# One eviction for two half banks, and a longer stretch for the preparation of later batches, in a fused attention and feed-forward kernel

## Chip, cores, metric

The kernel runs on one core of a Trainium2 chip. The metric is the device time of one execution in microseconds (us), as the median of several runs. A profile page comes from one of them.

## The reference, cut

```python
B, N, C = 4, 6080, 256              # attention over channels, four batches
qn = q / (norm(q, axis=1) + 1e-6);  kn = k / (norm(k, axis=1) + 1e-6)
s  = kn.transpose(0, 2, 1) @ qn / tau            # "gram" product, 256 x 256 per batch
a  = softmax(s, axis=-1)
x  = v @ a                                       # 24320 x 256
h  = x @ w_in                                    # 256 -> 2048
g  = s_ * relu(h)**2 + b_
out = g @ w_out                                  # 2048 -> 256
```

## The kernel before

The kernel folds `a @ w_in` into one matrix `wa` per batch, so that a group of 512 rows needs `v @ wa`, relu, square and the product with `w_out`. There are 48 groups, and each takes 16 passes of the main loop, which this text calls **half-slots**. A half-slot issues two matmuls of 512 columns for group g and seven of 128 columns for group g - 1.

The product with `w_out` is done with seven quarter products in place of eight (a scheme like Strassen's). Four of them (1, 3, 5, 7) accumulate in one half of a PSUM bank called X, and the bank YZ holds Y in one half and Z in the other. VectorE evicts a partial sum (reads it out of PSUM) after each product. The code is cut, and the comments are added:

```python
        def p1():                                   # after product 1 (bank X)
            st["u1"] = U()
            evacuate(st["u1"], st["X"], rowconst[:, lo], 1)
        def p5():                                   # after product 2 (half Z)
            st["u5"] = U()
            evacuate(st["u5"], st["Z"], rowconst[:, hi], 1)
        def p6():                                   # after product 3 (bank X, accumulated)
            st["u2"] = U()
            evacuate(st["u2"], st["X"], rowconst[:, hi], 1)
        def p2():                                   # after product 4 (half Y)
            evacuate(out_sb(0, lo), st["Y"], st["u1"], 2)
        def p7():                                   # after product 5 (bank X)
            evacuate(out_sb(1, hi), st["X"], st["u5"], 2)
        def p3():                                   # after product 6 (half Z, accumulated)
            evacuate(out_sb(0, hi), st["Z"], st["u2"], 2)
            ...
        def p4():                                   # after product 7 (bank X)
            evacuate(out_sb(1, lo), st["X"], rowconst[:, lo], 1)
            ...
        products = [
            ("X", G(0, 0), W[:, 0, :, lo], p1),
            ("Z", lambda: S[1], T1, p5),
            ("X", lambda: S[2], T2, p6),            # may start only when p1 has read X
            ("Y", G(1, 0), W[:, 1, :, lo], p2),
            ("X", lambda: S[3], T3, p7),
            ("Z", lambda: S[4], W[:, 1, :, hi], p3),
            ("X", G(1, 1), N4, p4),
        ]
```

VectorE also makes the operand sums S1 to S4, and three quarters of the squares (`g<-r`); each of these instructions takes 1.2 us. The places within a group of 16 half-slots are fixed. Counted in half-slots from the start of group g, for the products of group g - 1: S1 at 2, S2 at 3, p1 at 5, S3 at 6, p5 at 7, p6 at 9, S4 at 10, p2 at 12, p7 at 14, p3 at 16, p4 at 18. The squares of VectorE stand at 8, 12 and 16, those of ScalarE at 3 and 5. A place 16 is place 0 of the next group.

Between these, batches 1 to 3 are prepared while the batch before is computed. The gram product of a batch takes 12 chunks of 4 pairs of matmuls. Each chunk brings one ScalarE square and, on VectorE, a square (`sq<-qk`) and two folds (`f<-sq`, `f<-f`). Then 18 finishing steps make `wa` (code cut, comments added):

```python
    FIN = (0, 3, 5, 7, 9, 11, 13, 17, 19, 22)   # copy, norms, 4 x inverse, scale, exp, exp, sums
    for b in range(1, B):
        gr = grams[b]
        w0 = first_group[b - 1] * FT + (26 if b == 1 else 6)
        w1 = first_group[b] * FT - 3
        fin_len = 54
        span = (w1 - fin_len) - w0 - 12
        n = NCH * JC
        for c in range(NCH):
            sc = w0 + span * c * JC / n
            ...
            for j in range(JC):
                at_step(w0 + span * (c * JC + j) / n, lambda gr=gr, c=c, j=j: gr.mm(c, j))
            def norm_step(gr=gr, c=c, sc=sc):
                ops = gr.norm_ops(c)             # ScalarE square, VectorE square, two folds, add
                for i, f in enumerate(ops):
                    at_step(int(sc) + 2 + 1 + i * 3, f)
            at_step(sc + 1, norm_step)
        ...                                      # the finishing steps start at w1 - fin_len + 1
```

## Time and profile before

| | before |
|---|---|
| time, median of 6 runs | 718.98 us |
| span of the profiled run | 717.3 us |
| TensorE busy | 695.1 us (97%) |
| VectorE busy | 623.7 us (87%), 877 instructions |
| ScalarE busy | 545.1 us (76%) |
| stops of TensorE in the main loop | 2.67 us (VectorE 1.08, ScalarE 1.59) |

A **stop**, here and below, is the time by which two successive matmul starts lie further apart than is usual for the shape of the first (0.056, 0.109 and 0.216 us for 128, 256 and 512 columns); all such excesses above 0.015 us are added up from the first matmul of the main loop on. A stop is put down to the engine whose instruction released the second matmul.

### The profile page before, as it was taken

What the parts mean: (1) busy time and instruction counts of PE and PEld (TensorE: products, weight loads), DVE (VectorE), ACT (ScalarE), POOL (GpSimd) and SP (SyncE); (2) the same over time, 40 slices, a digit from 0 to 9 for tenths busy, and PEclk for the clock granted to TensorE, in tenths of its full rate; (3) what the DMA queues carried; (4) which work ended last, traced back from release to release, by engine and by line L of the source; (5) the groups of instructions that cost most, each with busy time, mean ns of one, the idle gap of its engine ahead of it and who ended that gap; (6) DMA issues with size and microseconds to landing.
All of it is one profiled execution on the core that took longest, in us unless ns stands there. A gap on an engine that the chain in (4) does not pass through costs nothing.

```text
span 717.3 us, 17484 instructions
## 1 busy us (share of the span) xinstructions
PE 695.1 (97%) x7417; PEld 502.9 (70%) x7417; DVE 623.7 (87%) x877; ACT 545.1 (76%) x593; POOL 110.7 (15%) x189
## 2 busy tenths in 40 slices
PE   4599999999999999999999999999999999999998
PEld 2456777776677777777677777777668777777777
DVE  4879999988789999998889899998887888888886
ACT  5779877787777777778777778777877777777875
POOL 4532323102101222111010222110000000000000
PEclk9999999999999999999999999999999999999999
DMA  9999999636555988444763887953323333321201
GB/s 235 208 258 173 151 154 160 112 100 123 116 109 118 135 137 144 110 91 90 132 149 59 139 141 122 152 94 75 100 63 75 93 71 75 96 60 45 83 31 74
DMA packets 87198, 83.47 MB, mean 116 GB/s; under 512 B 56304, under 2 KB 62000, under 8 KB 87120
## 3 DMA queue, kind: packets, MB, share of 16 engines
q0 software_dynamic: 26352, 43.40, 38.5%
q1 hardware_dynamic: 60192, 37.64, 21.9%
q8 instruction: 58, 0.95, 0.6%
q10 hardware_dynamic: 576, 1.31, 0.5%
q14 instruction: 20, 0.16, 0.1%
HBM read 78.91 MB, written 24.90 MB: 145 GB/s over the span
## 4 chain that ended last, share of the span: by engine, by line
PE 92%; DMA 4%; DVE 2%; ACT 2%; issue 0%; DVEq 0%; ACTq 0%
PE h_ps L661 45%; PE o_ps L829 40%; PE s_ps L148 4%; PE wa_ps L329 2%; DMA qk<-in_k_dram 1%; DMA raw<-in_q_dram 1%; DMA w_in<-in_moe_w_in_dram 1%; PE o_ps L733 1%; ACT sq L177 1%; ACT r L671 1%; DVE f L191 1%; PE o_ps L707 0%; DVE sq L174 0%; DVE o_sb L689 0%; DVE S L758 0%
## 5 line engine op out<-in xcount | busy, mean ns | idle before, releaser
L671 ACT ACTIVATE r<-h_ps 128x1024 f16<-128x1024 f32 (+1 forms) x384 | 388.3, 1014 | 151.2 <-PE h_ps L661 147.5
L661 PE MATMUL h_ps<-vT,wa 128*128 128x512 f16 (+7 forms) x1632 | 452.0, 364 | 0.5 <-ACT r L671 0.4
L829 PEld LDWEIGHTS <-S 128*128 128x128 f16 x2944 | 198.0, 98 | 84.7 <-issue 0.2
L829 PEld LDWEIGHTS <-g 128*128 128x128 f16 x2208 | 155.1, 98 | 74.1
L684 DVE TENSOR_TENSOR g<-r 128x2048 f16<-128x2048 f16 (+2 forms) x150 | 174.6, 1164 | 14.5 <-ACT r L671 13.9
L829 PE MATMUL o_ps<-T,S 128*128 128x128 f16 x2208 | 183.3, 219 | 0.1
L661 PEld LDWEIGHTS <-wa 128*128 128x128 f16 x1632 | 136.0, 98 | 20.3 <-DVE wa L324 0.7
L829 PE MATMUL o_ps<-w_out,g 128*128 128x128 f16 x1472 | 134.2, 219 | 0.2 <-DVE u L689 0.2
L689 DVE SCALAR_TENSOR_TENSOR o_sb<-o_ps,s_out,u 128x256 f32<-128x256 f32 x138 | 66.3, 481 | 50.9 <-PE o_ps L829 48.7
L682 ACT ACTIVATE g<-r 128x1024 f16<-128x1024 f16 (+1 forms) x97 | 100.4, 1035 | 0.2
L148 PE MATMUL s_ps<-qk 128*128 128x256 f16 (+1 forms) x384 | 70.2, 283 | 16.0 <-ACT qk L139 9.5
L388 POOL DMA_DIRECT2D v<-in_v_dram x48 | 30.9, 648 | 264.9 <-DMA vT<-v 197.7
L689 DVE SCALAR_TENSOR_TENSOR u<-o_ps,s_out,rowconst 128x256 f32<-128x256 f32 x138 | 65.7, 476 | 0.0
L829 PE MATMUL o_ps<-w_out,S 128*128 128x128 f16 x736 | 63.5, 219 | 0.0
L829 PE MATMUL o_ps<-N,g 128*128 128x128 f16 x736 | 63.4, 219 | 0.0
L207 POOL DMA_DIRECT2D f<-f x30 | 26.3, 876 | 224.4 <-DVE f L191 182.5
L758 DVE TENSOR_TENSOR S<-S,g 128x2048 f16<-128x2048 f16 (+1 forms) x47 | 56.4, 1200 | 1.3
L177 ACT ACTIVATE sq<-qk 128x1024 f16<-128x1024 f16 (+2 forms) x53 | 54.5, 1041 | 3.9 <-DMA qk<-in_k_dram 2.3
L756 DVE TENSOR_TENSOR S<-g 128x2048 f16<-128x2048 f16 (+1 forms) x47 | 56.0, 1192 | 0.0
L762 DVE TENSOR_TENSOR S<-g,S 128x2048 f16<-128x2048 f16 x46 | 55.9, 1214 | 0.0
L760 DVE TENSOR_TENSOR S<-g 128x2048 f16<-128x2048 f16 x46 | 55.8, 1214 | 0.0
L148 PEld LDWEIGHTS <-qk 128*128 128x128 f16 (+1 forms) x384 | 32.2, 101 | 22.0 <-ACT qk L139 10.0
(85 smaller groups left out, 313.8 us busy)
## 6 DMA issues: line engine op xcount, KB each, us to landing
out_dram<-o_sb SPq DMA_DIRECT2D x42, 512.0 KB, 3.0
v<-in_v_dram POOLq DMA_DIRECT2D x47, 256.0 KB, 4.6
qk<-in_k_dram POOLq DMA_DIRECT2D x42, 256.0 KB, 6.2
qk<-in_q_dram POOLq DMA_DIRECT2D x42, 256.0 KB, 7.1
f<-f POOLq DMA_DIRECT2D x30, 128.0 KB, 3.2
vT<-v SPq DMA_TRANSPOSE x182, 3.1
out_dram<-o_sb SPq DMA_DIRECT2D x10, 256.0 KB, 4.5
w<-in_moe_w_out_dram POOLq DMA_DIRECT2D x4, 512.0 KB, 9.6
```

The lines of the kernel that those rows point to most:

```text
L148: po(nc.tensor.matmul(self.s_ps[:, ch, :], qc[:np_, j, ts(ch, P)], kc[:np_, j, :], start=(c == 0 and j == 0 and ch == 0), stop=(c == len(s ...
L177: po(nc.scalar.activation(out=st["sq"][:np_, a, js, :], in_=(qc, kc)[a][:np_, js, :], func=AF.Square))
L661: po(nc.tensor.matmul(dst, wa[:, ci, ts(m, P)], src, start=(ci == 0), stop=(ci == CH - 1), skip_group_check=True))
L671: po(nc.scalar.activation(out=r16[:, :, i % 2, :n], in_=h_tiles.pop((g, i))[:, :, :n], func=AF.Relu))
L682: po(nc.scalar.activation(out=dst, in_=src, func=AF.Square))
L684: po(nc.vector.tensor_mul(dst, src, src))
L689: po(nc.vector.scalar_tensor_tensor(out=dst, in0=src, scalar=s_out, op0=ALU.mult, in1=add, op1=ALU.add))
L756: po(nc.vector.tensor_add(T[1], A21, A22))
L758: po(nc.vector.tensor_sub(T[2], T[1], A11))
L760: po(nc.vector.tensor_sub(T[3], A11, A21))
L762: po(nc.vector.tensor_sub(T[4], A12, T[2]))
L829: po(nc.tensor.matmul(st[name][:, j, :], a()[:, i, ts(j, P)], w[:, i, :], start=first, stop=last, skip_group_check=True))
```

## The change

Two things are meant to relieve VectorE, which is 87% busy. First, Y and Z are evicted together, as one bank of 512 elements after product 6, which saves one instruction per group; the u buffers are widened for that, and a fold of batch 0 takes its buffer from another pool. Second, the finishing steps of batches 1 to 3 start ten half-slots later (54 becomes 44), batch 1 starts four later (26 becomes 30), and the gram products and their squares and folds are spread over the longer stretch.

```diff
--- before.py
+++ after.py
@@ -75,7 +75,7 @@
     rpool = pool("rpool", 2)
     gpool = pool("gpool", 2)
     spool = pool("spool", 1)
-    upool = pool("upool", 4)
+    upool = pool("upool", 2)
     opool = pool("opool", 2)
 
     ps_gram = pool("ps_gram", 1, space=PSUM)
@@ -218,7 +218,7 @@
             if at_end:
                 def half(a):
                     if "h" not in st:
-                        st["h"] = late_pool.tile([P, 2, 2, C], FP16, tag="h", name="h")
+                        st["h"] = sq_pool.tile([P, 2, 2, C], FP16, tag="f2", name="h")
                     po(nc.vector.tensor_add(st["h"][:np_, a], st["sq"][:np_, a, :2],
                                             st["sq"][:np_, a, 2:]))
                     self.rows[a].append((st["h"], np_, 2))
@@ -601,10 +601,10 @@
                 at_step((g - 2) * FT + 6, lambda g=g: crossbar_v(g))
     for b in range(1, B):
         gr = grams[b]
-        w0 = first_group[b - 1] * FT + (26 if b == 1 else 6)
+        w0 = first_group[b - 1] * FT + (30 if b == 1 else 6)
         w1 = first_group[b] * FT - 3
         NCH = len(gr.chunks)
-        fin_len = 54
+        fin_len = 44
         span = (w1 - fin_len) - w0 - 12
         n = NCH * JC
         for c in range(NCH):
@@ -766,7 +766,6 @@
         lo, hi = slice(0, P), slice(P, C)
         G = lambda h, t: lambda: g_tiles[g][:, h, :, ts(t, TG // 2)]
         W = w_out16.rearrange("p (i h) c -> p h i c", h=2)
-        U = lambda: upool.tile([P, 2, P], FP32, tag="u", name="u")
 
         def out_sb(t, half):
             if g not in o_sbs:
@@ -774,25 +773,25 @@
             return o_sbs[g][:, ts(t, 2), half]
 
         def p1():
-            st["u1"] = U()
-            evacuate(st["u1"], st["X"], rowconst[:, lo], 1)
+            st["u"] = upool.tile([P, 2, C], FP32, tag="u", name="u")
+            evacuate(st["u"][:, :, lo], st["X"], rowconst[:, lo], 1)
 
         def p5():
-            st["u5"] = U()
+            st["u5"] = upool.tile([P, 2, P], FP32, tag="u5", name="u5")
             evacuate(st["u5"], st["Z"], rowconst[:, hi], 1)
 
         def p6():
-            st["u2"] = U()
-            evacuate(st["u2"], st["X"], rowconst[:, hi], 1)
+            evacuate(st["u"][:, :, hi], st["X"], rowconst[:, hi], 1)
 
         def p2():
-            evacuate(out_sb(0, lo), st["Y"], st["u1"], 2)
+            pass
 
         def p7():
             evacuate(out_sb(1, hi), st["X"], st["u5"], 2)
 
         def p3():
-            evacuate(out_sb(0, hi), st["Z"], st["u2"], 2)
+            out_sb(0, lo)
+            evacuate(o_sbs[g][:, 0:2, :], st["YZ"], st["u"], 2)
             if g in HALVES:
                 store(g, 0, 2)
 
@@ -806,7 +805,7 @@
             if name == "X":
                 st["X"] = halves[0]
             else:
-                st["Z"], st["Y"] = halves
+                st["YZ"], st["Y"], st["Z"] = t, t[:, :, lo], t[:, :, hi]
 
         products = [
             ("X", G(0, 0), W[:, 0, :, lo], p1),
```

## The prediction

> **What bounds the kernel now.** I read the page's busy shares first, then the chain that ended last, then who waited for whom, then the groups by form, and last the timeline of TensorE instruction by instruction.
>
> ```profile
> PE 695.1 (97%) x7417; PEld 502.9 (70%) x7417; DVE 623.7 (87%) x877; ACT 545.1 (76%) x593; POOL 110.7 (15%) x189
> PE 92%; DMA 4%; DVE 2%; ACT 2%; issue 0%; DVEq 0%; ACTq 0%
> ```
>
> TensorE is busy 97% of a span of 717.3 us, and 92% of the chain that sets the end is matmuls. VectorE, the engine that the change relieves, is at 87% but has only 2% of that chain. A busy TensorE can still hide waits inside its modelled ends, so the waits and the timeline must confirm it:
>
> ```profile
> ACT r L671 <- PE h_ps L661: 147.5, 238, 1.1
> DVE o_sb L689 <- PE o_ps L829: 54.0, 71, 1.3
> DVE g L684 <- ACT r L671: 13.9, 34, 0.8
> ```
>
> ScalarE stands idle 147.5 us for TensorE, VectorE 54.0 us: both wait for TensorE, hardly the reverse. The steady state, TensorE only (start in us, duration in us):
>
> ```profile
> 403.95 0.59 PE L661 MATMUL h_ps<-vT,wa 128*128 128x512 f16 x2
> 404.38 0.55 PE L829 MATMUL o_ps<-T,S 128*128 128x128 f16 x7
> 404.77 0.59 PE L661 MATMUL h_ps<-vT,wa 128*128 128x512 f16 x2
> 405.20 0.55 PE L829 MATMUL o_ps<-T,S 128*128 128x128 f16 x7
> ```
>
> Two matmuls of 512 columns take 0.43 us from their start to the next start, seven of 128 columns take 0.39 us. That is 0.215 and 0.056 us each, and the half-slot (one pass of the main loop) is 0.82 us. I added up, over all matmuls, how much the distance from one start to the next exceeds the usual one of its shape (0.056, 0.109, 0.216 us for 128, 256, 512 columns). From 38.2 us on, when the main loop runs, the excess is only 2.7 us. Of it 1.08 us ends with a VectorE eviction, in seven places, and about 1.5 us with ScalarE (0.56 of that at 43.97 us, before anything that the change touches). Half of VectorE's part lies in one place, the first group of seven products:
>
> ```profile
> 70.31 0.80 PE L829 MATMUL o_ps<-T,S 128*128 128x128 f16 x7
> 70.25 0.48 DVE L689 SCALAR_TENSOR_TENSOR u<-o_ps,s_out,rowconst 128x256 f32<-128x256 f32 x1
> 72.72 0.48 DVE L689 SCALAR_TENSOR_TENSOR u<-o_ps,s_out,rowconst 128x256 f32<-128x256 f32 x1
> ```
>
> The first row took 0.80 instead of 0.55 us, a stop of 0.25 us, because the eviction at 70.25 us was late. After the one at 72.72 us another 0.37 us is lost. The rest is 0.08 us at 140, 0.12 at 249, 0.11 at 421, 0.14 at 704, and 0.02 at 87 us.
>
> **What the Trainium skill says.** TensorE: Matmul & The Clock Gate, section "Wait — 56ns, not 53.3ns?": a warm matmul starts N/2.4 GHz plus about 2.5 ns after the last, 55.6 and 215.7 ns for 128 and 512 columns. The trace agrees (56 and 216 ns): in steady state there is no slack left in TensorE's stream. VectorE: DVE Perf Modes, section on the TRN2 errata, gives 120 cycles plus one per element at 0.96 GHz for PSUM to SBUF: 392 ns for 256 elements, 658 ns for 512. The recorded durations are longer, 481 and 747 ns in the rows below, but neighbours overlap: the eviction at 70.25 us is followed by the next start at 70.65, 0.40 us later, and two of 512 elements from 64.20 us are followed at 65.52, 0.66 us each. So spacing agrees with the page. PSUM — Partial Sum Buffer, section "PSUM bank collisions raise a hardware error", asks to guard PSUM by bank, not by address. The program does so: before, the sixth product (half Z) waits for VectorE's read of half Y of the same bank.
>
> **The change part by part.**
>
> 1. The merged eviction. Halves Y and Z of one PSUM bank were read by two instructions of 256 elements, and are now read by one of 512 after the sixth product.
>
> ```profile
> L689 DVE SCALAR_TENSOR_TENSOR o_sb<-o_ps,s_out,u 128x256 f32<-128x256 f32 x138 | 66.3, 481 | 50.9 <-PE o_ps L829 48.7
> L689 DVE SCALAR_TENSOR_TENSOR u<-o_ps,s_out,rowconst 128x256 f32<-128x256 f32 x138 | 65.7, 476 | 0.0
> L689 DVE SCALAR_TENSOR_TENSOR o_sb<-o_ps,s_out,rowconst 128x512 f32<-128x512 f32 x2 | 1.4, 747 | 0.1
> ```
>
> 138 is 3 for each of 46 groups; it becomes 1 of 256 and 1 of 512 for each group, so VectorE has 46 instructions fewer. By spacing a group saves 2 x 0.395 - 0.66 = 0.13 us, 46 x 0.13 = 6.0 us. By recorded durations it is 0.481 x 2 - 0.747 = 0.215 us, 9.9 us. Busy time is a union of intervals, so its fall lies between: I expect VectorE at 614 to 618 us. On the path to the end none of this counts by itself. It counts only through the 1.08 us of stops. The compiled order also shows that 45 of TensorE's waits, those of the sixth product on the Y eviction, disappear. The trace has no stop at any of them, so that is worth 0.
>
> 2. Buffers. The u buffers become two of double width plus two for u5, and the fold of the first batch's late chunk borrows a buffer of another pool. A u buffer is reused two groups later, some 27 us, so no new wait. The borrowed buffer is used once, in program order on VectorE. 0 us.
>
> 3. Later preparation. From the loop's arithmetic: batch 1's gram products before run from half-slot 26, one pair each 81/48 = 1.69 half-slots; after from 30, each 87/48 = 1.81. Batches 2 and 3: each 117/48 = 2.44, after 127/48 = 2.65. The number of matmuls is unchanged (7417 on the page), and TensorE is the bound, so spreading them saves nothing of their 0.109 us each. What it does is to thin out the accompanying squares and folds: each chunk costs VectorE 0.68 + 0.68 + 0.42 us by duration and ScalarE one square of 1.05 us. Over the 85 us from 65 to 150 us VectorE was busy 81.57 us, or 96%. There a late eviction can stop TensorE, and here it is 7% fewer chunks per time. In the first group of seven products the square of about 0.6 us (by spacing) moves behind the first two sums in the compiled order, and its fold of 0.6 us moves behind the second u eviction. But TensorE also arrives earlier there, since about three gram pairs of 0.22 us no longer stand before it: VectorE gains 1.2 us where TensorE gains 0.65. So I expect the 0.25 + 0.37 us to shrink to about 0.3.
>
> Sum. VectorE's stops: 1.08 us down to about 0.5, -0.6 us. ScalarE's stops after the start: two of 0.175 us (at 263 and 436 us, the same place of the pattern in batches 2 and 3) depend on how squares fall against the half-slots, and shift; I take half away, -0.2 us. The warm-up stretch from 56 to 61 us, where ScalarE had no idle time and stopped TensorE by 0.22 + 0.12 + 0.13 us, loses gram matmuls that filled its time; I leave it at 0. The tail: the longer eviction falls near 710.5 us where VectorE waits anyway, 0. Together -0.8 us: 719.0 - 0.8 = **718.2 us**.
>
> **The rivals.** VectorE as a hidden bound: were its 87% what limits, 6 to 10 us of less work would give up to 1.4%. For it: 96% in the dense stretch. Against it: 54.0 us of idle time waiting for products, and 1.08 us of stops in all. I take that rival's ceiling as 1.1 us, which gives 717.9. ScalarE in the warm-up: gram pairs that move out of a stretch in which TensorE waits for ScalarE leave it standing, and have to be done later; four pairs are 0.87 us, so at worst some 719.5 us. For it: ScalarE is busy 6.00 of 6.00 us from 54 to 60 us. Against it: from 61 to 66 us it has idle time of 0.64 and 0.42 us for TensorE. Late folding: the last fold of the weights of batches 1 to 3 now comes in the first half-slot of the group that needs them, 10 later. It is used by the thirteenth half-slot, some 12 x 0.82 = 9.8 us later, against an eviction of 0.745 us and a VectorE queue of 2 or 3 us. If it were too late, three boundaries of perhaps 1 us would give 721. The wider eviction could also delay the square behind it by 0.27 us; VectorE waited 1.2 to 1.3 us just before that eviction (idle time at 182.54 and 197.00 us), so I see no stop.
>
> **Range and chances.** The best case removes nearly all stops of both kinds within reach, about 1.7 us: 717.3. The bad case is new alignments that add half a microsecond: 719.3. Two per cent is 14.4 us, five times all stops of the loop, so faster or slower by that is next to excluded: 0.01 each, within 0.98.
>
> **What would show it.** TensorE's count of matmuls and its start-to-start distances unchanged; VectorE 46 instructions fewer and busy 614 to 618 us; one 128x512 eviction with u as input, x46, near 747 ns; the stops near 70 and 73 us smaller; idle time of VectorE for products larger than 54.0 us in sum, since freed time turns into waiting. Wrong it would be if stops appear at the batch boundaries (near 196, 369 and 541 us), if gram loads come late, or if the first matmul of the main loop moves from 38.2 us.

## The result

The changed kernel takes **724.21 us** (median of 6 runs, 724.13 to 724.37) against 718.98 us (718.83 to 719.09). The ratio is 1.0073, with a 95% interval of 1.006 to 1.0086: 5.2 us slower, and outside the predicted range of 717.3 to 719.3. (Ratios here are the mean time of one kernel's fast runs over that of the other's of the same rounds, so not quite the ratio of the medians quoted.)

The page of the changed kernel, its busy shares and its chain by engine:

```profile
PE 698.0 (97%) x7417; PEld 503.5 (70%) x7417; DVE 617.7 (86%) x831; ACT 545.3 (75%) x593; POOL 110.8 (15%) x189
PE 85%; DVE 5%; ACT 5%; DMA 3%; issue 1%; DVEq 0%; ACTq 0%
```

VectorE has 46 instructions fewer and 6.0 us less to do, as intended, and the matmuls are as many as before. But the chain that sets the end is now TensorE for 85% instead of 92%, with 5% each of VectorE and ScalarE, which had 2%. Work was removed and waits were added. The waits and the group of the merged eviction:

```profile
DVE o_sb L689 <- PE o_ps L828: 61.3, 81, 1.5
ACT r L671 <- DVE o_sb L689: 10.1, 12, 0.8
L689 DVE SCALAR_TENSOR_TENSOR o_sb<-o_ps,s_out,u 128x512 f32<-128x512 f32 x46 | 34.5, 750 | 47.5 <-PE o_ps L828 47.5
```

The merged eviction takes 750 ns, and VectorE stands idle 47.5 us in all, 1.03 us each time, just before it. That is the first hint: the work that was saved had filled a hole, and what takes its place starts when the hole ends.

TensorE's stops in the main loop are 7.95 us, against 2.67 before: 5.28 us more, which is the whole loss of 5.23 us. VectorE's part rose from 1.08 to 3.59 us, ScalarE's from 1.59 to 4.36 us. One of the two largest stops for VectorE is at 321 us (0.48 us; its like in batch 3, at 496 us, is 0.49). TensorE there (start, duration):

```profile
320.19 0.59 PE L661 MATMUL h_ps<-vT,wa 128*128 128x512 f16 x2
320.62 0.39 PE L828 MATMUL o_ps<-T,S 128*128 128x128 f16 x4
321.32 0.33 PE L828 MATMUL o_ps<-T,S 128*128 128x128 f16 x3 [0.32 <-DVE u L689]
```

Four matmuls of product 2 are done at 320.62 + 4 x 0.056 = 320.84 us, and the first of product 3 starts at 321.32: a stop of 0.48 us for p1, which must have read bank X. VectorE in the same stretch:

```profile
315.01 0.75 DVE L689 SCALAR_TENSOR_TENSOR o_sb<-o_ps,s_out,u 128x512 f32<-128x512 f32 x1 [1.49 <-PE o_ps L828]
315.67 1.22 DVE L684 TENSOR_TENSOR g<-r 128x2048 f16<-128x2048 f16 x1
316.81 0.69 DVE L174 TENSOR_TENSOR sq<-qk 112x1024 f16<-112x1024 f16 x1
317.41 0.48 DVE L689 SCALAR_TENSOR_TENSOR o_sb<-o_ps,s_out,rowconst 128x256 f32<-128x256 f32 x1
317.80 1.21 DVE L756 TENSOR_TENSOR S<-g 128x2048 f16<-128x2048 f16 x1
319.05 1.23 DVE L758 TENSOR_TENSOR S<-S,g 128x2048 f16<-128x2048 f16 x1
320.19 0.68 DVE L191 TENSOR_TENSOR f<-sq 112x1024 f16<-112x1024 f16 x1
320.80 0.47 DVE L689 SCALAR_TENSOR_TENSOR u<-o_ps,s_out,rowconst 128x256 f32<-128x256 f32 x1
```

VectorE was idle 1.49 us, because the merged eviction has to await product 6. Then it works without a gap for 6.3 us, up to the end of p1 at 321.27 us. This is its **tight stretch**: it begins when product 6 ends, and product 3 of the next products waits at its end. The merged eviction (0.66 us to the next start, where half Z alone took 0.40), a square of the gram (0.60) and a fold (0.61) stand in it. What VectorE could save elsewhere in the group does not help here. In the kernel before, the same group had no gram work in the stretch, and p1 was done at 318.16 us, before product 3 could start at 318.41 + 4 x 0.056 = 318.63 us:

```profile
317.68 0.48 DVE L689 SCALAR_TENSOR_TENSOR u<-o_ps,s_out,rowconst 128x256 f32<-128x256 f32 x1
318.41 0.55 PE L829 MATMUL o_ps<-T,S 128*128 128x128 f16 x7
```

The second kind of stop is at the end of the preparation. ScalarE and TensorE around 349 us of the changed kernel (eT are the exponentials, r_ps their sums):

```profile
346.66 0.50 ACT L302 ACTIVATE eT<-sm_t,rNone 128x256 f16<-128x256 f32 x1
347.06 1.01 ACT L671 ACTIVATE r<-h_ps 128x1024 f16<-128x1024 f32 x1
347.96 1.05 ACT L682 ACTIVATE g<-r 128x1024 f16<-128x1024 f16 x1
348.91 0.50 ACT L302 ACTIVATE eT<-sm_t,rNone 128x256 f16<-128x256 f32 x1
349.10 0.17 PE L312 MATMUL r_ps<-parts,eT 128*128 128x1 f16 x1
349.47 0.23 PE L312 MATMUL r_ps<-parts,eT 128*128 128x1 f16 x3 [0.21 <-ACT eT L302]
```

The finishing steps moved by ten half-slots, and with it their places within a group: the two exponentials now stand at half-slots 3 and 5, where ScalarE also has its two squares. The second one starts at 348.91 us, and TensorE, which needs it for the sums, stops 0.34 us. Before the change the same steps stood at half-slots 9 and 11, and there was no stop: the second exponential began 1.7 us ahead of the sums.

```profile
336.30 0.50 ACT L302 ACTIVATE eT<-sm_t,rNone 128x256 f16<-128x256 f32 x1
338.04 0.24 PE L312 MATMUL r_ps<-parts,eT 128*128 128x1 f16 x4
```

The stop comes once for each of batches 1 to 3, three times in all.

The third kind is the warm-up of the loop, from 38 to 80 us, where the stops grew from 1.86 us (0.62 of it for VectorE) to 2.61 us, all of it for ScalarE.

### The profile page after: what moved, and what is told of

Same layout as the page of the kernel before. It is cut to its first block, busy times and chain, and to the rows that moved or that the text cites.

```text
span 722.4 us, 17410 instructions
## 1 busy us (share of the span) xinstructions
PE 698.0 (97%) x7417; PEld 503.5 (70%) x7417; DVE 617.7 (86%) x831; ACT 545.3 (75%) x593; POOL 110.8 (15%) x189
## 4 chain that ended last, share of the span: by engine, by line
PE 85%; DVE 5%; ACT 5%; DMA 3%; issue 1%; DVEq 0%; ACTq 0%
PE h_ps L661 41%; PE o_ps L828 37%; PE s_ps L148 4%; PE wa_ps L329 2%; ACT r L671 2%; ACT g L682 1%; DMA qk<-in_k_dram 1%; DMA raw<-in_q_dram 1%; DMA w_in<-in_moe_w_in_dram 1%; DVE f L191 1%; DVE S L758 1%; DVE S L756 1%; ACT sq L177 1%; DVE o_sb L689 1%; DVE g L684 1%
## 5 line engine op out<-in xcount | busy, mean ns | idle before, releaser
L689 DVE SCALAR_TENSOR_TENSOR o_sb<-o_ps,s_out,u 128x256 f32<-128x256 f32 x92 | 56.7, 616 | 60.5 <-PE o_ps L828 60.4
```

The source lines that it names most:

```text
L689: po(nc.vector.scalar_tensor_tensor(out=dst, in0=src, scalar=s_out, op0=ALU.mult, in1=add, op1=ALU.add))
```

## Experiments

All are correct, and timed against the kernel before on the same chip (its median was 718.9 to 719.0 us each time). The table also gives the stops; the last column is what the stops alone would explain. The 95% intervals of the ratio include 1 for a3, b1, c2 and d2, and that of a1 begins at 1.000; but no run of any version was as fast as the slowest run of the kernel before in the same rounds, and the traces name the stops.

| run | us | longer than before | stops: all, VectorE, ScalarE | stops more than before |
|---|---|---|---|---|
| before | 718.98 | | 2.67, 1.08, 1.59 | |
| changed | 724.21 | 5.23 | 7.95, 3.59, 4.36 | 5.28 |
| a1 merge only | 719.92 | 1.05 | 3.65, 2.06, 1.59 | 0.98 |
| a2 schedule only | 722.43 | 3.56 | 6.15, 1.81, 4.34 | 3.48 |
| a3 start 30 only | 719.80 | 0.93 | 3.50, 0.76, 2.73 | 0.83 |
| a4 end 44 only | 721.59 | 2.72 | 5.20, 2.06, 3.14 | 2.53 |
| b1 later, not spread | 720.05 | 1.06 | 3.74, 1.11, 2.63 | 1.07 |
| b2 end 38 | 720.34 | 1.35 | 4.12, 1.57, 2.55 | 1.45 |
| b3 sums later | 724.50 | 5.51 | 8.33, 3.62, 4.70 | 5.66 |
| b4 half Y late | 721.39 | 2.40 | 4.90, 3.30, 1.60 | 2.23 |
| c1 work moved | 722.11 | 3.10 | 5.91, 2.81, 3.10 | 3.24 |
| c2 merge, work moved | 720.02 | 1.01 | 3.73, 0.63, 3.10 | 1.06 |
| d1 exponentials moved | 723.69 | 4.79 | 7.48, 4.16, 3.32 | 4.81 |
| d2 merge, moved, third buffer | 719.52 | 0.62 | 3.23, 1.01, 2.21 | 0.56 |
| e1 only VectorE and ScalarE work spread | 721.47 | 2.49 | see text | |
| e2 only matmuls spread | 720.37 | 1.39 | 4.14, 1.34, 2.80 | 1.47 |

In every row the stops, which are from one profiled run each, account for the time to within 0.2 us. The question is therefore only which edit makes which stop.

### Which part: a1 to a4

a1 has the buffers and the merged eviction of the change with the old schedule. a2 to a4 have the old evictions:

```diff
# a2: both lines;  a3: the first alone;  a4: the second alone
-        w0 = first_group[b - 1] * FT + (26 if b == 1 else 6)
+        w0 = first_group[b - 1] * FT + (30 if b == 1 else 6)
-        fin_len = 54
+        fin_len = 44
```

Expected of a1:

> The merged eviction (with its buffers) on the old schedule. Measured so far: before 719.0, changed 724.2 us; stops of TensorE in the main loop 2.7 us before, about 8.1 after. Theory P (placement: the eviction of half Y used to run in idle time of VectorE, the merged one lengthens VectorE's tightest chain, from the end of the sixth product to the third product of the next group, by 0.27 us): stops of the third product (o_ps<-T,S) for the u eviction in the dense gram stretches, total about 720.5 to 722. Theory S (the schedule alone makes the loss): 718.5 to 719.2, stops for VectorE not above 1.1 us.

Expected of a2:

> The schedule part alone (start 30, end 44), with separate evictions. Theory P: only the stops that wait for ScalarE and the three of 0.34 us at the sums after the exponentials remain, about 1.2 + 1.0 us more than before, 720.5 to 721.5. Theory S: all of the loss, 723.5 to 724.5.

Expected of a3:

> Only the first start 26 to 30. Both theories: only the stretch from 56 to 78 us changes, in the changed kernel its stops grew from about 1.3 to 2.1 us (those for ScalarE by 1.3, while two for VectorE went), so about +0.5 to +1.0 us: 719.5 to 720.0, the batches 2 and 3 as before.

Expected of a4:

> Only the later end (54 to 44). Both theories: three stops of 0.34 us at the sums product for the exponentials (near 175, 349, 523 us), +1.0 us. Theory P: nothing more beyond 0.3 us, 719.8 to 720.3. Theory S: also the stops of the third product for u near 290 to 325 and 465 to 500 us, 721.5 to 723.

The merge alone costs 1.05 us, which lies between the ranges of the two theories. The schedule alone costs 3.56 us, between them too; most of that, 2.72 us, is the later end (a4, in the range of theory S), and the later start is 0.93 us. So both theories were half right: the merge does cost, but the schedule costs three times as much. The two parts add up to 4.61 us, less than the 5.23 us together. Among the stops that only the two together make are four of 0.16 us (at 233, 262, 407 and 437 us), which neither a1 nor a4 has; the next section returns to them.

What the merge does shows best where the kernel before did not stop. Product 2 near 276 us, in a1:

```profile
276.14 0.48 DVE L689 SCALAR_TENSOR_TENSOR u<-o_ps,s_out,rowconst 128x256 f32<-128x256 f32 x1
276.28 0.72 PE L828 MATMUL o_ps<-T,S 128*128 128x128 f16 x7
```

and the same seven matmuls in the kernel before:

```profile
275.86 0.55 PE L829 MATMUL o_ps<-T,S 128*128 128x128 f16 x7
```

0.72 against 0.55 us is a stop of 0.17 us for an eviction that ends at 276.62 us. In batch 1 there are two more of the kind, at 87 us (0.016 before, 0.284 in a1; the difference is the 0.26 to 0.27 us by which the merged eviction is longer than that of half Z) and at 102 us (none before, 0.265 in a1).

a3 has most of its loss where it was expected. The four half-slots without gram matmuls at 60 us leave TensorE waiting for relus: a stop of 0.49 us at 60.5 us instead of 0.13, and in the first group of seven products 0.43 and 0.30 us for ScalarE near 73 and 75 us instead of stops for VectorE. But of its 0.83 us of stops only 0.52 us lies there. 0.27 us more lies at 141 us, where product 7 waits for an eviction (0.35 us instead of 0.08), and that was not expected. The rival of the prediction named the warm-up, with at worst 719.5 us; a3 is 719.80.

### Later or more spread: b1, e1, e2

a4 moves the end and spreads the gram work. b1 moves the end only:

```diff
-        fin_len = 54
-        span = (w1 - fin_len) - w0 - 12
+        fin_len = 44
+        span = (w1 - 54) - w0 - 12
```

Expected:

> Separate evictions, start 26, the finishing steps ten half-slots later, but the gram products kept at their old places (not spread). Later end alone cost 721.6 with the spread. Theory R (resonance: with a spread of 127 half-slots over 12 chunks three chunks take two groups, so that the square and the first fold of a chunk fall into VectorE's tight stretch in every second group, with fewer gram matmuls there to delay TensorE): the stops of the third product near 290 and 320 us are gone, the three of 0.34 us for the exponentials stay: 719.9 to 720.4. Rival L (a later end is bad as such): still 721 or more.

720.05 us, within the expectation of theory R. Its stops differ from those of the kernel before by just three, of 0.34 us each, at the sums of the exponentials. So of the 2.72 us of the later end, 1.06 us comes from the finishing steps, and about 1.6 us from spreading (1.66 with each run against its own runs of the kernel before, 1.54 by the two times). By the traces a4 has 1.46 us more stops than b1: 0.91 in four stops of product 3 in batches 2 and 3, 0.37 in two more relu stops, 0.25 in one stop at 148 us. The text that follows explains the first.

Why does spreading harm? The spread over 127 half-slots gives 10.58 half-slots per chunk, so three chunks take 31.75 half-slots, nearly two groups of 16. From the loop's arithmetic the square and the first fold of a chunk then fall on half-slots 0 or 1 and 3 or 4 in groups 13, 15, 17 and 19 of batch 2, and in the four that correspond in batch 3. That is 1.2 us of extra work (0.60 + 0.61 by spacing) in the tight stretch. Before, with 9.75 half-slots per chunk, only one group of each of these batches (16 and 28) had as much. But TensorE also arrives later where gram pairs stand between product 6 and product 3, 0.218 us for each pair. Groups 13 and 15 have three such pairs and do not stop in a4; group 17 has two and stops 0.12 us, group 19 has one and stops 0.33 us:

```profile
319.06 0.39 PE L829 MATMUL o_ps<-T,S 128*128 128x128 f16 x4
319.61 0.33 PE L829 MATMUL o_ps<-T,S 128*128 128x128 f16 x3 [0.17 <-DVE u L689]
```

The sum in the following expectation was fitted to the two stops of a4 and then asked about runs that had not been made.

e1 and e2 separate the two, with an own span for the squares and folds (so) and for the matmuls (sc). The edit is cut; both also set `fin_len` to 44:

```diff
+        span_ops = (w1 - OPS) - w0 - 12            # e1: OPS 44, matmuls 54; e2: OPS 54, matmuls 44
+            so = w0 + span_ops * c * JC / n
-            at_step(max(3, sc - 16), lambda gr=gr, c=c: gr.load(c))
+            at_step(max(3, min(sc, so) - 16), lambda gr=gr, c=c: gr.load(c))
-            def norm_step(gr=gr, c=c, sc=sc):
+            def norm_step(gr=gr, c=c, sc=so):
-            at_step(sc + 1, norm_step)
+            at_step(so + 1, norm_step)
```

Expected of e1:

> End 44 and start 26 with separate evictions; gram matmuls at their old places, the squares and folds spread. From the stops of end 44 alone, a sum: stop of the third product = (VectorE's gram work in half-slots 0 to 5) - 0.218 x (gram pairs in half-slots 0 to 7) - 0.645 us, which gives its 0.12 us (1.2 us of work, 2 pairs) and 0.33 us (1.2 us, 1 pair). Here: nothing at the stop near 290 us (3 pairs) and about 0.55 us near 319 and 492 us (1.2 us of work, no pair). Theory R (places of the squares and folds): 721.2 to 721.8. Rival T (thinner matmul stream): about 720.05 as with neither spread.

Expected of e2:

> The reverse: squares and folds at their old places, the gram matmuls spread. By the same sum no stop of the third product above 0.02 us in batches 2 and 3 (at most 0.2 us in batch 1 near 102 us). Theory R: 720.0 to 720.4. Rival T: 721.3 to 721.8.

e1 takes 721.47 us (721.36 without its profiled run, see below) and e2 720.37 us, both as theory R says. In e1 the stop near 290 us is gone, and the one near 319 us is larger than a4's 0.33 us:

```profile
320.70 0.39 PE L831 MATMUL o_ps<-T,S 128*128 128x128 f16 x4
321.41 0.33 PE L831 MATMUL o_ps<-T,S 128*128 128x128 f16 x3 [0.32 <-DVE u L691]
```

From 320.70 + 4 x 0.056 to 321.41 us it is 0.48 us, and 0.06 us were lost just before at S1; together 0.54 us, where the sum had said 0.55. In e2 no product 3 in batches 2 and 3 stops, and the one new stop of a product 3 in batch 1 is 0.24 us, at 101.6 us (the sum had said at most 0.2). So it is the place of the squares and folds of VectorE that costs, and gram matmuls in the same stretch hide it. A thinner stream of matmuls alone costs little: e2 lies 0.3 us above b1. (The profiled run of e1 took 723.08 us, 1.7 us more than the median of its three other runs. In it TensorE's granted clock was 0.50 from 38 to 41 us: the loop began 0.4 us later, and its first eight matmuls took 1.2 us longer. So its stops are not in the table; without these eight they are 4.99 us, 2.32 more than before.)

The sum also fits stops that it was not made for. The merged eviction puts 0.26 us more into the tight stretch. For the changed kernel this makes 0.16, 0.16, 0.38 and 0.60 us for groups 13, 15, 17 and 19; the trace has 0.16, 0.17, 0.37 and 0.59 us (the last two with a stop at S1 just before). So the four stops that neither part has alone are those of groups 13 and 15, and their like in batch 3: with three pairs, only both changes together are too much. For a1 it makes 0.16 us in groups 16 and 28, where the trace has 0.17. This was worked out afterwards, but with no new constant.

### Places, not lateness: b2, b3, d1

b2 ends 16 half-slots later than before, even later than the change, so that the finishing steps stand on their old places in the group. Batches 2 and 3 also start two half-slots later, which the expectation puts down to the single gram bank; no run shows that need.

```diff
-        w0 = first_group[b - 1] * FT + (26 if b == 1 else 6)
+        w0 = first_group[b - 1] * FT + (26 if b == 1 else 8)
-        fin_len = 54
+        fin_len = 38
```

Expected:

> Separate evictions, start 26, end 38 instead of 54 (and batches 2 and 3 start 2 half-slots later, which the single gram bank needs): later and more spread than in the change, but 16 half-slots later than before, so that the finishing steps fall on the same places of the group as before. Theory R (places in the group decide, not lateness): no stop at the sums for the exponentials, at most two stops of about 0.12 us for u, 718.8 to 719.6. Rival L: more than the 721.6 us of end 44.

The three stops for the exponentials are gone, and in batches 2 and 3 there are two of 0.12 us for u, as theory R said. But the time is 720.34 us, 0.7 us above the expected range, since other places changed too: eight stops of product 6 for the eviction of half Y, 0.66 us in all with one of 0.38, 0.4 us more in the warm-up, and two relu stops of 0.18 us more. Lateness as such is refuted (that rival had it above 721.6); but each new spacing finds its own collisions. In batch 1 of b2 two chunks take almost one group (8.08 half-slots each), and by the loop's arithmetic the square and the first fold stand in the tight stretch in six groups in a row, but with four gram pairs beside it. After the first of these groups (0.27 us at 71 us) no product 3 stops there. So meeting the tight stretch again and again cost time here only where too few gram matmuls stood beside it.

b3 leaves the exponentials of the changed kernel where they are and moves the sums behind them:

```diff
-    FIN = (0, 3, 5, 7, 9, 11, 13, 17, 19, 22)
+    FIN = (0, 3, 5, 7, 9, 11, 13, 17, 19, 24)
```

Expected:

> The changed kernel with the sums product (and the folds behind it) two half-slots later, so that ScalarE, which has a relu and a square ahead of the second exponential, is done. Theory: the three stops of 0.34 us go, 724.2 - 1.0 = 723.2 us, the others stay. Rival (another engine or the bank is what it waits for): 724.2.

This failed: 724.50 us. The stop moved. Near 351 us in b3:

```profile
350.28 0.22 PE L828 MATMUL o_ps<-w_out,g 128*128 128x128 f16 x1
350.79 0.59 PE L661 MATMUL h_ps<-vT,wa 128*128 128x512 f16 x2 [0.30 <-ACT r L671]
```

The next matmul starts 0.51 us after the last instead of 0.056, so TensorE now stops 0.46 us for the relu which stands behind the second exponential. The sums were only the first to meet ScalarE's backlog. d1 moves the exponentials themselves to half-slots 8 and 10 of the group:

```diff
-    FIN = (0, 3, 5, 7, 9, 11, 13, 17, 19, 22)
+    FIN = (0, 3, 5, 7, 9, 11, 13, 22, 24, 27)
```

Expected:

> The changed kernel with the two exponentials moved from half-slots 3 and 5 of a group, where ScalarE also has a relu and a square each, to 8 and 10, and the sums and folds behind them. Moving only the sums (b3) had traded three stops of 0.34 us for three of 0.46 us at the next relu. Theory: it is ScalarE's own backlog of two relus, two squares and two exponentials; with the exponentials elsewhere both kinds of stop go, 724.2 - 1.0 = 723.2 us. Rival (the sums product wait for something else, or the stop moves again): 724.0 to 724.6.

723.69 us, and both kinds of stop are gone; the sums near 353 us run as four together again:

```profile
350.60 0.52 ACT L302 ACTIVATE eT<-sm_t,rNone 128x256 f16<-128x256 f32 x1
353.10 0.24 PE L312 MATMUL r_ps<-parts,eT 128*128 128x1 f16 x4
```

But only half of the 1.0 us is gained: the last finishing steps (the products that fold `w_in` into `wa`) now come five half-slots later, and stop TensorE at one of them (0.07 us, three times) and at the first gram matmul of the next batch, which needs the bank of the last of them (0.18 us, twice). So the cause of this stop is settled, and the rest of its gain was lost to waits that the trace names.

### Where an eviction stands: b4, c1, c2, d2

b4 keeps two separate evictions, and only moves that of half Y to that of half Z:

```diff
         def p2():
-            evacuate(out_sb(0, lo), st["Y"], st["u1"], 2)
+            pass
         def p3():
+            evacuate(out_sb(0, lo), st["Y"], st["u1"], 2)
             evacuate(out_sb(0, hi), st["Z"], st["u2"], 2)
```

Expected:

> The old schedule and separate evictions, but that of half Y moved to that of half Z, so two of 256 elements (0.79 us by spacing) in place of one of 512 (0.66 us) behind the sixth product. Theory P (place: work moved from idle time of VectorE into its tight stretch): worse than the merged one (719.9) by about 0.13 us in each of its six or seven stops for u, 720.4 to 721.0. Rival F (the wide instruction or its strided u buffer is what costs): as before, 718.8 to 719.2.

It takes 721.39 us, slower than the merged one and somewhat more than expected. The stop at 277 us is 0.27 us (0.17 in a1, 0 before), that at 87 us 0.38 us (0.28, 0.02). The row at 277 us takes 0.82 us, where a1 had 0.72 and the kernel before 0.55:

```profile
277.04 0.82 PE L830 MATMUL o_ps<-T,S 128*128 128x128 f16 x7
```

So it is neither the wide instruction nor its buffer: the cost of a1 comes from moving Y's work into the tight stretch, and merging even saves a part of it.

c1 and c2 try the opposite, and clear the tight stretch of gram work. c1 is the kernel before, c2 is a1, both with this (comments added):

```diff
+                last = 0
                 for i, f in enumerate(ops):
-                    at_step(int(sc) + 2 + 1 + i * 3, f)
+                    t = int(sc) + 2 + 1 + i * 3
+                    if 0 < i < 4:                       # VectorE's square and folds
+                        m = t % FT                      # half-slots 0-2 to 6, 3-5 to 9
+                        t = max(last, t - m + 6 + m // 3 * 3 if m < 6 else t)
+                        last = t
+                    at_step(max(last, t), f)
```

Expected of c1:

> The kernel before with VectorE's squares and folds of later batches moved out of half-slots 0 to 5 of a group (0 to 2 go to 6, 3 to 5 to 9). Theory P/R (the stretch from the end of the sixth product to the third product of the next group is VectorE's tight one): the stops for u in gram stretches go (about 0.8 of 1.08 us), 718.0 to 718.6. Rival: no place is better than another, 719.0, or stops appear at the fourth to seventh product, 719.5.

Expected of c2:

> The merged eviction on the old schedule (719.9) with the same move of squares and folds. Theory P: the merged eviction costs only where this work shares its stretch, so its loss goes: 718.0 to 718.8. Rival F (the wide instruction costs as such): 719.0 to 719.6, stops for u in every group.

c1 failed: 722.11 us. The stops for u in the gram stretches are gone, but now product 6 waits for Y's eviction p2, at half-slot 12 (0.26, 0.86 and 0.49 us in batch 1), because the moved work stands ahead of it:

```profile
110.22 0.38 PE L835 MATMUL o_ps<-w_out,S 128*128 128x128 f16 x4 [0.70 <-DVE o_sb L695]
```

In c2, where that eviction is no longer there, batches 2 and 3 have not one stop for VectorE left. Here the merge is worth 722.11 - 720.02 = 2.1 us. So the sign of the merged eviction depends on what else stands around it. But c2 missed its expectation too: 720.02 us, not 718.0 to 718.8, and not faster than the kernel before; nor does it have the stops for u in every group of rival F. One new stop of 0.88 us stood at 78 us, where TensorE waited for a cast on ScalarE, and ScalarE had waited for VectorE:

```profile
75.80 1.06 ACT L177 ACTIVATE sq<-qk 128x1024 f16<-128x1024 f16 x1 [0.77 <-DVE f L191]
```

The theory was a buffer of squares that a later fold had not freed. d2 is c2 with a third one:

```diff
+    sq3_pool = pool("sq3_pool", 3)
-                        st["sq"] = (late_pool if at_end else sq_pool).tile(
+                        st["sq"] = (late_pool if at_end else sq3_pool).tile(
```

Expected:

> The merged eviction, the old schedule, squares and folds of VectorE moved out of half-slots 0 to 5, and a third buffer for the squares. c2 (two buffers) had no stop for u or S left after 80 us but two of 0.88 and 0.18 us near 73 to 78 us, where ScalarE stood 0.77 us waiting for a buffer of squares that VectorE's later fold had not freed. Theory: with a third buffer the 0.88 us stop goes: 720.0 - 0.9 = 719.1, between 718.5 and 719.3, about as before. Rival (ScalarE is simply overfull there): 720.0.

719.52 us, 0.5 us faster than c2 but short of the expected 718.5 to 719.3: the stop of 0.88 us is gone, and two others appeared (0.13 and 0.26 us at 78 and 80 us). No version beat the kernel before: the fastest run of d2 (719.32 us) is slower than the slowest of the kernel before in the same rounds (719.06). The 2.67 us of stops that the kernel before has are also all that this way could still give.

## Why the prediction was wrong, point by point

- **The bound: right.** TensorE's stream sets the time, the matmuls are as many as before, and the start of the loop stayed within 0.3 us of 38.2 us.
- **Step 1, cost of the merged eviction: right in size, wrong in effect.** VectorE is at 617.7 us (614 to 618 predicted), the eviction at 750 ns (747), its idle time for products rose from 54.0 to 61.3 us. The step that failed is the overlap in the last sentence of the rivals: the wider eviction delays the square behind it by 0.27 us, VectorE waited 1.2 to 1.3 us before it, "so I see no stop". The idle time ahead of the eviction was read as room. It is not: VectorE waits there for the same product 6, and a chain of some 6 us starts behind it. a1 measured +1.05 us (VectorE's stops 1.08 to 2.06), and b4 shows that it is the place.
- **Step 2, buffers: right.** a1 and the changed kernel have no stop for them. The 45 waits that vanish were worth 0 in the kernel before, as said; in c1 five of them cost 1.96 us.
- **Step 3, the schedule: wrong, and the largest part.** "What it does is to thin out" took the average density, 7% fewer chunks per time, as the measure. What decides is where in a group the work falls. The later end moved the exponentials onto ScalarE's squares (b1, +1.06 us; b3 and d1 show the backlog), and the spread put three chunks on two groups, so that 1.2 us of squares and folds met the tight stretch in every second group, in two of them per batch with too few gram matmuls (a4 less b1, about +1.6 us, of which 0.91 in these stops; e1 and e2 separate the two kinds of work). The prediction had computed 2.44 and 2.65 half-slots per pair, which contains this, but did not lay the chunks over the 16 places.
- **The sum.** The term "VectorE's stops: 1.08 us down to about 0.5" measured 3.59, "-0.2 us" for ScalarE's stops measured +2.8. The -0.6 us did not follow from the working either: its part 3 takes 0.62 to about 0.3, which is -0.3, and names nothing for the other -0.3. VectorE's stops at 70 and 73 us did go, as said (a3), but stops for ScalarE took their place.
- **The signs.** Those named for being wrong (stops at the batch boundaries, late gram loads, a moved start of the loop) did not come. The one that told was in the list of what would show it right: start-to-start distances of TensorE unchanged.
- **The range.** Its bad case was "new alignments that add half a microsecond", one tenth of what came. It was scaled to the stops that were there, not to those that a shift of the finishing steps and of 36 chunks could make. That more than 2% either way was next to excluded was right.
- **Late folding: rightly rejected.** There is no stop at the batch boundaries in the changed kernel.
- The Trainium skill had the relevant hint, in Perfetto Trace Analysis, section "Optimizing Scalar/DVE Operations": larger operations can help "if the engine is saturated", and where an engine is not saturated but causes bubbles on others, "breaking up instructions may allow work to be completed sooner". a1 agrees: merging saves 0.13 us of VectorE's time per group, but in a chain that waits for the later of its two inputs it added 0.26 us. b4 adds a condition: broken up, but with both pieces at the late place, it is slower than a1 (+2.40 against +1.05 us). It is the earlier start of half Y that helped here, not the smaller instructions.

What stays open: how much of the 0.52 us that a3 loses in the warm-up is the missing gram matmuls and how much the shifted ScalarE squares was not separated, and its 0.27 us at 141 us was not examined. The relu stops of 0.18 us in batches 2 and 3 (two in the kernel before and in b1, four in a4 and e2, none in e1) come and go with the places of the gram work; why was not examined further.

## What to carry to other kernels

In a tuned pipeline that is bound by one engine, ask of each saved instruction whether it stood in a hole or in a chain that ends at the bound engine; idle time just before an instruction is not room for it when a chain starts behind it. When periodic work is spread, lay its period over that of the loop: near a simple ratio (here 3 chunks on 2 groups) it can meet the same tight place again and again, and thinner on average was worse here. A sum of the distances between starts, by shape, found every microsecond of the loss, while the busy share stayed at 97%.

## What the Trainium skill lacked or had wrong

- VectorE: DVE Perf Modes gives 120 cycles plus one per element for an eviction from PSUM. The runs show that this is the spacing of starts (0.40 and 0.66 us for 256 and 512 elements), while the recorded durations are 0.48 and 0.75 us. The page does not say which of the two its PSUM figure is; Perfetto Trace Analysis does (about 125 ns on PSUM as engine-busy time, with part of the recorded latency overlapping with the next instruction). It says "about twice" for the recorded overhead, which would be some 250 ns. Here the recorded durations of 256 and 512 elements, 481 and 747 ns, differ by 266 ns, so some 215 ns of the 481 do not grow with the elements (an estimate from the two).
- Perfetto Trace Analysis, "Optimization Strategy", says to look for gaps between slices of the engine. Here the profile's gaps of TensorE before its seven products and before h_ps add up to 0.8 us before and 2.6 us after, while the distances between starts show stops of 2.67 and 7.95 us in the whole loop. Most waits sit in overlapping matmul records, and no page says to sum start distances by shape.
- No page warns that spreading work evenly can resonate with the loop's period: 10.58 half-slots per chunk against 16 gave stops of product 3 of 0.12 and 0.33 us in a4 where 9.75 gave none.
- TensorE: Matmul & The Clock Gate, section "What's actually happening", gives half the clock after an idle window of about 3.4 us. In one profiled run (e1) the granted clock was 0.50 from 37.6 to 41.0 us, though no gap between TensorE's records in the ten us before was longer than 1.3 us. Matmuls of 512 columns started 0.43 us apart there, and it cost that run some 1.6 us. Whether it lies behind any scatter of other runs was not looked into.
